# Attention mixed with a Mish network: the shifted copies of VectorE's exponential batches made in part by GpSimd, 1024 or 512 columns at a time

## The chip, the core and the metric

The kernel runs on one core of a Trainium2 chip. The metric is the device time of one execution, in microseconds, and lower is better. A run gives one such time; a kernel's figure is the median of its runs. Besides, one execution was taken by the hardware profiler; its page and its trace are what the numbers below come from. TensorE is called PE there (PEld is its weight load), VectorE DVE, ScalarE ACT, GpSimd POOL, and SP is the engine whose queue issues most DMAs.

## The reference

```python
def _A_ref(x, wqkv, wo):                       # x: 1 x 2048 x 640, 32 heads of 20
    qkv = (x @ wqkv).reshape(B, S, 3, H, Dh).transpose(2, 0, 3, 1, 4)
    scores = jnp.einsum("bhqd,bhkd->bhqk", q, k) * Dh ** -0.5
    p = softmax(scores)
    o = jnp.einsum("bhqk,bhkd->bhqd", p, v)
    return o.transpose(0, 2, 1, 3).reshape(B, S, D) @ wo
def _B_ref(x, w1, b1, w2):                     # w1: 640 x 1536
    h = x @ w1 + b1
    return (h * tanh(softplus(h))) @ w2
g = sigmoid((x * gate_w).sum(-1, keepdims=True))
out = g * _A_ref(...) + (1 - g) * _B_ref(...)  # both on the same x, bfloat16
```

The large part is the exponential of 32 x 2048 x 2048 scores.

## The kernel before

**Units and slots.** Scores are computed transposed, 128 keys by 512 queries of one head at a time; such a tile is a unit. A group is four heads (rows 0, 32, 64, 96 of the PE array) and one block of 512 queries. Three units make a slot, and there are 683 slots. For each slot PE writes three banks of PSUM (line 1324); two sets of three banks take turns, so the scores of slot s+2 can only be written when the exponentials of slot s have been read. ScalarE then makes the exponentials of a slot in one instruction (line 1345) into the ring ETS, and PE multiplies them with the values V, four heads at a time (line 1649), into one bank of sums per group.

**VectorE's units.** In some slots the third unit is not given to ScalarE. VectorE evicts it from PSUM instead (line 1391): it multiplies the score and adds a constant so that the result, stored as a 16-bit integer, is the bit pattern of an approximate exponential in f16. ScalarE's instruction of that slot then has 1024 columns in place of 1536. Four such units make a batch in a buffer of 2048 columns, called Y. To even out the error of the approximation, the batch is used three times: as it is (Y), with a constant subtracted from the integers (a copy in another buffer, U), and with a constant added (written over Y, called E; its values are multiplied by VW, a scaled copy of V made at line 1620). PE multiplies all three with V and adds them up. The two additions of a constant are the *shifts*. Before the change each shift is one VectorE instruction of 2048 columns (for batches of fewer units one of 1024 and/or one of 512), made by `shift` at line 1429. The buffers have the names of what else lies there: PADS, KT, QT, OTN, HB, REG, W2R.

**What else VectorE does.** It evicts projections, hidden units (line 1035) and outputs (line 1148) from PSUM, copies each group's sums to OUNG (line 1809), multiplies them by the broadcast reciprocals (line 1765) and computes Mish in eight steps on U (lines 1082 and 1085).

**GpSimd.** At the start it clears buffers. Later it makes the reciprocals of each group's sums, RR to the power of -1 (line 1831), which wait for a DMA that gathers the sums from OUNG; a DMA stores them in SUMS and four more spread them over BCT. In a few groups it also does the multiplication by the reciprocals.

**What sets the order.** All instructions come from one planner, written in Python, which runs when the kernel is built. It keeps a clock for each engine, adds instructions with an assumed cost each (the constants at the top of the file) and so fixes the order on every engine; nothing is decided on the chip. Dependences become semaphore waits, and each engine works through its queue in order. `choose(s)` decides whether slot s gives a unit to VectorE: it compares VectorE's planned backlog, and a correction from the table NUDGE for every eight slots, with limits (BEHIND, IDLE, and so on). `work` fills VectorE's planned gaps from lists of waiting jobs, `soon` among them, which holds the shifts; `settle` (line 493), called after each eviction, looks whether a job of `blend` (a Mish step) or `norm` (the multiplication by the reciprocals) can be given to GpSimd: only if it fits behind VectorE's last instruction of kind "L" (a shift, a Mish step or a multiplication, which work from SBUF to SBUF) and beside the evictions that follow in the plan. The job then waits for that last "L" instruction.

Of the kernel before, what the change touches and what calls it, by code (L numbers as in the profile page):

```python
# [11 lines left out]
I16 = mybir.dt.int16  # L12
# [27 lines left out]
OWE = -0.1  # L40
# [15 lines left out]
SPUN = 0.4  # L56
# [3 lines left out]
INVERT = 0.6  # L60
ASIDE = 1.3
ASIDE_1 = 1.2
APART = 0.1
AWAIT = 0.01
SHARE = 0.3
AWAIT_1 = 0
CALM_END = 60
# [3 lines left out]
LANES = 2  # L71
TAKEN = 3.6
LATE_OFF = 0.4
# [6 lines left out]
GIVE_BACK = 50  # L80
IDLE = 5
IDLE_2 = 6
# [3 lines left out]
NEAR = 0.2  # L86
STORED = 1.0
TALL = 0.1
BEYOND = 0.6
# [7 lines left out]
SPREAD = 1  # L97
# [3 lines left out]
BEHIND = 8  # L101
PATIENCE = 3
CATCH_UP = 10
BUSY = 0.9
CROWD = 1.05
MARGIN = 2.5
EAGER = 90
LOAD = 1.0
MISH = 4
GROUP = 2.5  # L110
LAST = 0
END = 55
SHIFT = 0.5
LAG = 40
SPARE = 3
WINDOW = 4.0
CALM = 1
# [10 lines left out]
OVER = 0.2  # L128
DIRECT = 3
FEW = 4  # L130
PART_DUE = 18
LAST_DUE = 13
# [21 lines left out]
NUDGE = [0.8, -4.2, -3.5, -3.7, 0.7, -0.7, -3.7, -1.5, -6, -1.5, -1.5, 2.3, 0.7, 0, -3.7, -1.5, 6, 0.0, 6, 0.7, -0.7, -5.9, 0.1, -0.7, 0, 3.7, -3, 1.5, 0.7, 0.7, 2.2, 6, 3.7, 1.5, 1, 2.2, 0.7, 2.1, 2.9, 2.3, 1.5, 6, 0.0, 2.9, 1.5, 0.7, -2.3, 1.5, 1.5, 1.5, 1.5, -2.3, 1.5, 0, 1.5, 0.8, 5, 0.0, 0.7, 2.9, 0.7, 1.5, 0, 4.5, 6, 0.7, -1.4, 1.6, 3, 0.8, 2.4, -0.8, 3.8, 0.0, 2.2, 5.7, 0.7, 5.2, 6, 0.7, 4.5, 0, 1.5, -0.7, -3, -1.5, -3]  # L154
# [116 lines left out]
def bass_gated_mix__softmax_full_mha__dense_activation_mish__prompt_kernel(  # L271
# [153 lines left out]
    def attention(pl, fast):  # L425
# [67 lines left out]
        def settle():  # L493

            while fast:
                for todo in (blend, norm):
                    job = todo[0][5] if todo and len(todo[0]) > 5 else None
                    ready = job and job[0]()
                    if not ready:
                        continue  # L500
                    line = pl.line
                    i = len(line)
                    while i and not line[i - 1][2]:
                        i -= 1
                    begin = max(ready.t1 + HOP, pl.now["pool"], line[i - 1][0])
                    while i < len(line) and line[i][0] <= begin:
                        i += 1
                    if begin + job[1] + APART <= pl.now["dve"]:
                        todo.popleft()
                        job[2](line[i - 1][1])  # L510
                        break
                else:
                    return
# [5 lines left out]
        def load(job):  # L519

            return job[0] * (SHARE if len(job) > 5 else 1)
# [5 lines left out]
        def work(until):  # L527
            while True:
                best = None
                lined = sorted([lane for lane in (*soon, blend) if lane], key=lambda lane: lane[0][3])  # L530
                for rank, todo in enumerate((norm, scaled, *lined, bg)):
                    for entry in todo if any(todo is lane for lane in soon) else islice(todo, 1):
                        cost, fn, dep = entry[:3]
# [874 lines left out]
        def close(batch):  # L1408
# [15 lines left out]
            where = spans(m)  # L1424
            each = QUAD * m / BATCH / len(where) + (0.0 if m == BATCH else 0.03)

            def shift(home, by, deps, after):
                for sp in where:
# [7 lines left out]
            def above():  # L1436
# [11 lines left out]
                def end(op):  # L1448
                    batch["parts"]["E"] = op
# [866 lines left out]
```

## Time and profile before

| what | value |
|---|---|
| median of 3 runs | 762.49 us (761.28 to 762.76) |
| the profiled execution's own time | 761.24 us |
| its span, first to last instruction | 759.4 us |
| instructions | 19104 |
| granted clock of TensorE | 0.999 |
| data read from and written to HBM | 35.57 MB, 7.51 MB (57 GB/s over the span) |

The span and the time of the same execution differ by 1.8 us. The page gives the busy time of each engine, groups of instructions by source line (busy time, mean duration of one, idle time of the engine ahead of them and what ended it), and the chain of waits that ended last. Other views of the same trace group by shape, cut the span into windows, or list instructions in order of time. An instruction's duration runs from its start to its end; on VectorE and ScalarE the next one can start before the last one has ended, so what one instruction takes from an engine that is never idle is the distance from its start to the next start.

### The profile page before, as it was taken

The numbers are of one execution on the slowest core, as the hardware profiler recorded it, in microseconds if no ns is written. First come the engines' busy times: TensorE is split into PE (matmuls) and PEld (weight loads), VectorE is DVE, ScalarE is ACT, GpSimd is POOL, SyncE is SP. The second block draws the span as 40 slices with busy tenths as digits, with TensorE's granted clock in tenths as the row PEclk, the third lists the DMA queues.
The fourth block names the chain that finished last, engine by engine and source line by source line (L and its number), as shares of the span: only waits on it lengthen the run. The fifth ranks groups of instructions, "written<-read, shape, count | busy, mean of one in ns | idle before, by whom it ended". The sixth has DMA issues, their size and how long they took to land.

```text
span 759.4 us, 19104 instructions
## 1 busy us (share of the span) xinstructions
PE 709.3 (93%) x7865; PEld 265.0 (35%) x7907; DVE 705.9 (93%) x1306; ACT 743.6 (98%) x714; POOL 123.2 (16%) x60
## 2 busy tenths in 40 slices
PE   8999999999999999999999899999998999999996
PEld 4433334333322333323333333333333333333332
DVE  4788899899899999998999999999999999999995
ACT  6999999999999999999999999999999999999996
POOL 8111101021110121202211202121022100111000
PEclk9999999999999999999999999999999999999999
DMA  8311311221133322241213222023122112010101
GB/s 182 109 56 48 103 52 34 66 65 59 49 94 98 104 57 81 57 133 37 64 44 111 74 67 58 29 68 86 48 68 69 55 41 71 21 33 14 31 7 39
DMA packets 80544, 49.03 MB, mean 65 GB/s; under 512 B 24602, under 2 KB 76690, under 8 KB 80450
## 3 DMA queue, kind: packets, MB, share of 16 engines
q1 hardware_dynamic: 80338, 47.71, 22.3%
q8 instruction: 65, 1.06, 0.6%
q14 instruction: 29, 0.24, 0.1%
q0 software_dynamic: 112, 0.01, 0.0%
HBM read 35.57 MB, written 7.51 MB: 57 GB/s over the span
## 4 chain that ended last, share of the span: by engine, by line
ACT 89%; PE 7%; DVE 2%; DMA 1%; issue 1%; SPq 0%; POOL 0%; POOLq 0%
ACT ETS L1345 86%; PE PS L1324 2%; ACT REG L1058 2%; PE PS L1649 2%; PE PS L562 2%; ACT W2R L1058 1%; PE PS L2043 1%; DMA WOQ<-in_A_wqkv_dram 1%; DMA REG<-in_B_w_dram 0%; DVE QT L1391 0%; PE PS L837 0%; DVE U L1082 0%; PE PS L901 0%; DVE HB L2168 0%; DVE OTN L1429 0%
## 5 line engine op out<-in xcount | busy, mean ns | idle before, releaser
L1345 ACT ACTIVATE ETS<-PS 128x1024 bf16<-128x1024 f32 (+1 forms) x683 | 722.6, 1270 | 4.0 <-PE PS L1324 3.2
L1324 PE MATMUL PS<-QT,KT 32*128 32x512 bf16 (+1 forms) x2112 | 268.8, 378 | 25.1 <-ACT ETS L1345 18.2
L1831 POOL TENSOR_TENSOR RR<-RR,NEG 128x16 f32<-128x16 f32 x29 | 91.4, 3151 | 499.4 <-DMA RR<-OUNG 492.5
L1649 PE MATMUL PS<-ETS,V_all 128*21 128x512 bf16 (+1 forms) x1624 | 167.0, 375 | 0.5 <-ACT ETS L1345 0.5
L1324 PEld LDWEIGHTS PS<-QT,KT 32*128 32x128 bf16 x2112 | 67.5, 91 | 234.1 <-ACT ETS L1345 182.1
L562 PE MATMUL PS<-XB,REG 128*128 128x256 bf16 (+3 forms) x703 | 78.5, 296 | 8.7 <-DVE HB L1035 2.6
L1391 DVE TENSOR_SCALAR QT<-PS 128x512 int16<-128x512 f32 x114 | 77.4, 688 | 2.7 <-PE PS L1324 1.8
L1391 DVE TENSOR_SCALAR OTN<-PS 128x512 int16<-128x512 f32 x112 | 76.0, 689 | 1.9 <-PE PS L1324 1.4
L562 PE MATMUL PS<-W2R,HB 128*32 128x320 bf16 (+1 forms) x666 | 73.8, 300 | 1.1 <-DVE OUTT L1148 0.5
L1391 DVE TENSOR_SCALAR PADS<-PS 128x512 int16<-128x512 f32 x90 | 61.2, 689 | 4.8 <-PE PS L1324 4.3
L562 PEld LDWEIGHTS PS<-XB,REG 128*128 128x128 bf16 (+1 forms) x719 | 38.3, 96 | 40.9 <-issue 28.0
L1649 PEld LDWEIGHTS PS<-ETS,V_all 128*21 128x21 bf16 x1624 | 40.2, 90 | 29.2 <-issue 25.0
L1085 DVE TENSOR_TENSOR U<-U 128x1024 f16<-128x1024 f16 x72 | 49.6, 689 | 0.2
L562 PEld LDWEIGHTS PS<-W2R,HB 128*32 128x32 bf16 (+1 forms) x666 | 33.5, 97 | 31.5 <-issue 14.9
L1391 DVE TENSOR_SCALAR KT<-PS 128x512 int16<-128x512 f32 x51 | 34.5, 687 | 4.5 <-PE PS L1324 4.1
L1391 DVE TENSOR_SCALAR REG<-PS 128x512 int16<-128x512 f32 x51 | 34.6, 688 | 1.6 <-PE PS L1324 1.5
L1035 DVE TENSOR_TENSOR HB<-PS,B1T 128x512 bf16<-128x512 f32 x48 | 33.1, 689 | 1.4 <-PE PS L562 1.3
L1082 DVE TENSOR_SCALAR U<-U 128x1024 f16<-128x1024 f16 x72 | 30.6, 425 | 0.5
L1429 DVE TENSOR_SCALAR QT<-QT 128x2048 int16<-128x2048 int16 (+2 forms) x52 | 27.7, 552 | 0.5 <-PE PS L1649 0.4
L1649 PE MATMUL PS<-QT,V_all 128*21 128x512 f16 x240 | 27.9, 384 | 0.0
L562 PE MATMUL PS<-XB,WOQ 128*32 128x512 bf16 (+1 forms) x136 | 25.1, 382 | 2.6 <-issue 1.6
L1429 DVE TENSOR_SCALAR OTN<-OTN 128x2048 int16<-128x2048 int16 (+2 forms) x42 | 25.8, 621 | 0.6 <-PE PS L1649 0.5
(174 smaller groups left out, 771.8 us busy)
## 6 DMA issues: line engine op xcount, KB each, us to landing
REG<-in_B_w_dram SPq DMA_DIRECT2D x36, 320.0 KB, 3.2
BCT<-SUMS SPq DMA_DIRECT2D x116, 64.0 KB, 2.0
W2R<-in_B_w_dram SPq DMA_DIRECT2D x12, 320.0 KB, 3.3
KT<-KS SPq DMA_DIRECT2D x28, 128.0 KB
QT<-QS SPq DMA_DIRECT2D x112, 20.0 KB
QS<-WOQ SPq DMA_DIRECT2D x16, 128.0 KB, 1.8
KS<-OTN SPq DMA_DIRECT2D x16, 128.0 KB, 1.8
W2R<-in_B_w_dram SPq DMA_DIRECT2D x1, 1920.0 KB, 8.4
```

What stands on the lines that cost most here:

```text
L562: op = e.matmul(PS[at, bank, cols], w[:, at], x, start=start, stop=stop, **({"tile_position": (0, i * rows)} if parts > 1 else {}))
L1035: ev = dve(lambda e: e.tensor_tensor(hb, PS[:, bank, :].rearrange("p (i t) -> p i t", i=2), bias, ALU.add), [last, b_load, *guarded, *b_re ...
L1058: ex = pl.add("act", lambda e: e.activation(U, h, AF.Tanh, scale=0.5, bias=-MISH_AT), [ev, u_free[0]], cost=0.95)
L1082: return lambda e: e.tensor_scalar(dst, src, *ops)
L1085: return lambda e: e.tensor_tensor(dst, one, two, ALU.mult)
L1324: op = pl.add("pe", lambda e, i=i, g=real(g), tile=tile, j=j, cols=cols, c=c, of_q=of_q: e.matmul(scores(s)[:, i, cols], KT[32 * j:32 * j ...
L1345: e_op[s] = pl.add("act", lambda e: e.activation(EXPS[:, at:at + n, :], scores(s)[:, 0:n, :], AF.Exp, scale=SCALE, bias=LIFT if fast else ...
L1391: ev = dve_by(lambda e: e.tensor_scalar(block(batch["y"], n, I16), scores(s)[:, 2, :], SCALE * ULPS, BIAS, ALU.mult, ALU.add), [s_op[s], * ...
L1429: op = pl.add("dve", lambda e, sp=sp: e.tensor_scalar(some_of(home, sp, I16), some_of(y, sp, I16), by, None, ALU.add), deps, cost=each, ki ...
L1649: lasts[n] = pl.add("pe", lambda e, v=v, j=j, src=src[:, cols], of_q=of_q, count=count: e.matmul(PS[32 * j:32 * j + EW, bank, of_q], v, sr ...
L1831: r = (pl.add("pool", lambda e: e.tensor_tensor(RR[:, :], RR[:, :], NEG[:, :].to_broadcast([P, 16]), ALU.pow), [got, m_neg], cost=INVERT) ...
L2043: pl.add("pe", lambda e: e.matmul(PS[:, bank, :], k[:, 0:P], k, start=True, stop=True), [free], cost=PASS, kind="S")
```

## The change

The shift of a batch is now a job (`queue_shift`) that can be done in pieces. Its buffer is cut into pieces of 1024 columns (512 for an odd unit). `run` is VectorE's turn: it does all the pieces that are left, as one instruction of 2048 columns if none has been taken. `aside` is GpSimd's turn: called from `settle`, it takes one piece off the end, if it fits beside VectorE's planned evictions at an assumed cost of BESIDE (1.05) or, for 512 columns, BESIDE / 2 + MOVED. What a batch's U, Y and E wait for is now a list of instructions, since pieces may come from two engines. `beside` is the test that `settle` had inside it before.

Most of the planner's constants and the table NUDGE have other values too: among them the assumed cost of GpSimd's reciprocals (INVERT 0.6 to 2.9) and of the DMA behind it (2.8 to 0.7), four lists of shifts for two (LANES), the limits of `choose` (BEHIND 8 to 8.5, IDLE_2 6 to 7), the times by which the last output parts are due (PART_DUE, LAST_DUE), and DIRECT: of the last groups, two and not three have their sums turned over by VectorE's transposes; the third one goes by GpSimd's reciprocals and the DMAs.

```diff
-INVERT = 0.6
+INVERT = 2.9
+BESIDE = 1.05
+MOVED = 0.1
+WITHIN = 0.1
-LANES = 2
+LANES = 4
-IDLE_2 = 6
+IDLE_2 = 7
-BEHIND = 8
+BEHIND = 8.5
-DIRECT = 3
+DIRECT = 2
...
-NUDGE = [0.8, -4.2, -3.5, -3.7, 0.7, ...
+NUDGE = [0.8, -4.2, -3.5, -1.5, 1.4, ...
...
 in settle():
                 else:
-                    return
+                    for lane in soon:
+                        moved = next((entry for entry in lane if entry[4](entry, lane)), None)
+                        if moved:
+                            break
+                    else:
+                        return
+
+        def beside(ready, cost):
+            line = pl.line
+            i = len(line)
+            while i and not line[i - 1][2]:
+                i -= 1
+            begin = max(ready.t1 + HOP, pl.now["pool"], line[i - 1][0])
+            while i < len(line) and line[i][0] <= begin:
+                i += 1
+            return line[i - 1][1] if begin + cost <= pl.now["dve"] else None
...
-            def shift(home, by, deps, after):
-                for sp in where:
-                    op = pl.add("dve", lambda e, sp=sp: e.tensor_scalar(
-                        some_of(home, sp, I16), some_of(y, sp, I16), by, None, ALU.add), deps, cost=each, kind="L")
-                after(op)
+            def queue_shift(first, home, by, deps, ready, after):
+                left = [sp for a, b, c, d in spans(m) for sp in ([(n, n + 1, c, d) for n in range(a, b)])]
...
+                def emit(eng, sp, cost, more=()):
+                    state["ops"].append(pl.add(eng, lambda e: e.tensor_scalar(
+                        some_of(state["home"], sp, I16), some_of(y, sp, I16), by(), None, ALU.add),
+                        [*state["deps"], *more], cost=cost, kind="L"))
+                def run():
+                    begin()
+                    some = [(0, 2, 0, 2)] if len(left) == 2 and left[1][3] == 2 else list(left)
+                    for sp in some:
+                        emit("dve", sp, each * (sp[1] - sp[0]) * (sp[3] - sp[2]) / m + 0.03 * (len(some) > 1))
+                    after(state["ops"])
+                def aside(entry, lane):
+                    op = ready()
+                    n = left[-1][3]
+                    if op is False or op is None or n < 2 and not MOVED:
+                        return False
+                    cost = BESIDE if n == 2 else BESIDE / 2 + MOVED
+                    dep = beside(op, cost + WITHIN)
+                    if dep is None:
+                        return False
+                    begin()
+                    sp = left.pop()
+                    emit("pool", sp, cost, [dep])
+                    if not left:
+                        lane.remove(entry)
+                        after(state["ops"])
+                    return True
...
-                    SUMS.ap().rearrange("j (r a) -> (j r) a", a=16), RR[:, :]), [r, *spread_last], "nr1", cost=0.4, tail=2.8)
+                    SUMS.ap().rearrange("j (r a) -> (j r) a", a=16), RR[:, :]), [r, *spread_last], "nr1", cost=0.4, tail=0.7)
```

In the changed file the lines have other numbers: 1361 is ScalarE's exponentials (1345 before), 1407 VectorE's evictions of its units (1391), 1456 the shifts (1429), 1881 the reciprocals (1831), 1699 the product with V (1649), 1340 the scores (1324).

**ScalarE, the first slots.** Rows with 1536 columns are slots that ScalarE has whole, those with 1024 columns slots that give a unit to VectorE. Seven rows of ScalarE's program, from the eighteenth exponential on, before:

```order
L1345 ACTIVATE ETS<-PS 128x1024 x3
L1345 ACTIVATE ETS<-PS 128x1536
L1345 ACTIVATE ETS<-PS 128x1024
L1345 ACTIVATE ETS<-PS 128x1536
L1345 ACTIVATE ETS<-PS 128x1024
L1345 ACTIVATE ETS<-PS 128x1536
L1345 ACTIVATE ETS<-PS 128x1024
```

and now, at the same place:

```order
L1361 ACTIVATE ETS<-PS 128x1024 x3
L1361 ACTIVATE ETS<-PS 128x1536
L1361 ACTIVATE ETS<-PS 128x1024
L1361 ACTIVATE ETS<-PS 128x1536
L1361 ACTIVATE ETS<-PS 128x1024 x3
L1361 ACTIVATE ETS<-PS 128x1536
L1361 ACTIVATE ETS<-PS 128x1024 x2
```

Slots that were whole have become slots with a unit for VectorE. Over the program there are 492 exponentials of 1024 columns and 191 of 1536 now, 475 and 208 before, and 491 evictions of VectorE's units for 474.

**VectorE and GpSimd, the second batch's U.** The batch was gathered in HB and its shifted copy U goes to KT. VectorE's rows around it before (the casts are projections):

```order
L1391 TENSOR_SCALAR KT<-PS 128x512
L755 CAST WOQ<-PS 128x512
L1391 TENSOR_SCALAR KT<-PS 128x512
L1429 TENSOR_SCALAR KT<-HB 128x2048
L755 CAST OTN<-PS 128x512
L1391 TENSOR_SCALAR KT<-PS 128x512 x2
```

and now:

```order
L1407 TENSOR_SCALAR KT<-PS 128x512
L771 CAST WOQ<-PS 128x512
L1456 TENSOR_SCALAR KT<-HB 128x1024
L1407 TENSOR_SCALAR KT<-PS 128x512
L771 CAST OTN<-PS 128x512
L1407 TENSOR_SCALAR KT<-PS 128x512 x2
```

The other 1024 columns are GpSimd's. Its rows behind the start-up work, where before there stood five reciprocals in a row and nothing between them:

```order
L1456 TENSOR_SCALAR KT<-HB 128x1024
L1456 TENSOR_SCALAR PADS<-KT 128x1024
L1881 TENSOR_TENSOR RR<-RR,NEG 128x16
L1456 TENSOR_SCALAR KT<-KT 128x1024 x2
L1456 TENSOR_SCALAR PADS<-PADS 128x1024
L1881 TENSOR_TENSOR RR<-RR,NEG 128x16
L1456 TENSOR_SCALAR HB<-HB 128x1024
```

Over the program GpSimd has 96 shifts of 1024 columns, 23 of 512, 9 Mish steps of 1024 columns, 30 reciprocals (29 before) and 7 multiplications by reciprocals (10 before). VectorE has 107 shifts of 2048 columns, 156 of 1024 and 27 of 512; before it had 190, 66 and 56.

**PE, the reader of that copy.** HB is Y of the same batch; the waits name the engine by its semaphore (f_dve, f_pool, f_act). Before:

```order
L1649 MATMUL PS<-HB,V_all 21x512 [waits f_dve]
L1649 MATMUL PS<-HB,V_all 21x512 x3
L1649 MATMUL PS<-ETS,V_all 21x512 x4
L1649 MATMUL PS<-KT,V_all 21x512 x4
L1324 MATMUL PS<-QT,KT 128x512 [waits f_dve,f_act]
```

and now:

```order
L1699 MATMUL PS<-HB,V_all 21x512 x4
L1699 MATMUL PS<-ETS,V_all 21x512 x4
L1699 MATMUL PS<-KT,V_all 21x512 [waits f_pool]
L1699 MATMUL PS<-KT,V_all 21x512 x3
L1699 MATMUL PS<-ETS,V_all 21x512 x4
L1340 MATMUL PS<-QT,KT 128x512 [waits f_dve,f_act]
```

PE now waits for GpSimd in front of the copy's four products, and the next scores stand behind them. Over the program 111 of PE's rows and 49 of VectorE's name GpSimd's semaphore; before it was 3 and 10.

111 lines of the change are left out of this document (55 added, 56 removed).

## The prediction

> **What bounds the kernel now.** The first part of the page gives the busy shares, the fourth the chain of work that ended last.
>
> ```profile
> PE 709.3 (93%) x7865; PEld 265.0 (35%) x7907; DVE 705.9 (93%) x1306; ACT 743.6 (98%) x714; POOL 123.2 (16%) x60
> ```
>
> The first row alone is not enough, since three engines are above 90%. The chain decides:
>
> ```profile
> ACT 89%; PE 7%; DVE 2%; DMA 1%; issue 1%; SPq 0%; POOL 0%; POOLq 0%
> ACT ETS L1345 86%; PE PS L1324 2%; ACT REG L1058 2%; PE PS L1649 2%; PE PS L562 2%; ACT W2R L1058 1%; PE PS L2043 1%; DMA WOQ<-in_A_wqkv_dram 1%; DMA REG<-in_B_w_dram 0%; DVE QT L1391 0%; PE PS L837 0%; DVE U L1082 0%; PE PS L901 0%; DVE HB L2168 0%; DVE OTN L1429 0%
> ```
>
> 86% of the span is ScalarE's exponentials, one behind the other. ScalarE is idle for 759.4 - 743.6 = 15.8 us in all. The view by windows of 20 us shows where; its columns are PE, PEld, DVE, ACT, POOL, each with its count of instructions, then clock and DMA.
>
> ```profile
> 0.00:20.00 20.00, 16.46 (x166) 8.76 (x171) 9.88 (x22) 13.15 (x15) 16.82 (x18) 1.00 0.88 193
> 140.00:160.00 20.00, 17.49 (x165) 6.08 (x168) 18.80 (x33) 19.97 (x20) 2.90 (x1) 1.00 0.21 60
> 540.00:560.00 20.00, 19.10 (x225) 7.00 (x226) 20.00 (x39) 20.00 (x20) 3.01 (x1) 1.00 0.15 44
> 740.00:759.00 19.00, 12.75 (x214) 6.02 (x204) 11.69 (x24) 12.76 (x11) 0.00 (x0) 0.95 0.12 38
> ```
>
> 6.85 us of the 15.8 are in the first window and 6.24 in the last, before the first scores and behind the last exponential; under 3 us are left for the 720 us between. So a shorter kernel needs less work on ScalarE. The work can go to VectorE, but VectorE has no room either: in the window at 540 it is busy for all 20 us. That is why GpSimd, at 3 us of 20, matters.
>
> **What one unit is worth to ScalarE.** The groups of line 1345 by shape (count, busy time, mean of one in ns):
>
> ```profile
> L1345 ACT ACTIVATE ETS<-PS 128x1024 bf16<-128x1024 f32 x475 | 483.5, 1140 | 2.0 <-PE PS L1324 1.5
> L1345 ACT ACTIVATE ETS<-PS 128x1536 bf16<-128x1536 f32 x208 | 323.1, 1568 | 2.0 <-PE PS L1324 1.7
> ```
>
> A unit that leaves ScalarE shortens one instruction from 1568 to 1140 ns, by 0.428 us. Both shapes overlap the next instruction in the same way, so the difference of the means is what the engine gains. The changed program has 492 exponentials of 1024 columns for 475: 17 units more, **17 x 0.428 = 7.3 us less on ScalarE**. The 24 Mish instructions of ScalarE are as before.
>
> **What VectorE pays and saves.** Here starts are needed, not durations. Instructions in order of time, VectorE's first, then GpSimd's one in that stretch, then a second stretch of VectorE:
>
> ```profile
> 164.38 0.68 DVE L1391 TENSOR_SCALAR W2R<-PS 128x512 int16<-128x512 f32 x1
> 164.98 0.42 DVE L1429 TENSOR_SCALAR QT<-HB 128x1024 int16<-128x1024 int16 x1
> 165.31 0.69 DVE L1391 TENSOR_SCALAR W2R<-PS 128x512 int16<-128x512 f32 x1
> 165.91 0.68 DVE L755 CAST WOQ<-PS 128x512 bf16<-128x512 f32 x1
> 166.51 0.68 DVE L1391 TENSOR_SCALAR W2R<-PS 128x512 int16<-128x512 f32 x1
> 167.11 0.42 DVE L1429 TENSOR_SCALAR HB<-HB 128x1024 int16<-128x1024 int16 x1
> ...
> 165.54 1.27 POOL L1765 TENSOR_TENSOR OTN<-OUNG,BCT 128x512 bf16<-128x512 f32 x1 [7.62 <-issue]
> ...
> 531.19 0.69 DVE L1429 TENSOR_SCALAR OTN<-OTN 128x2048 int16<-128x2048 int16 x1
> 531.79 0.29 DVE L1429 TENSOR_SCALAR REG<-QT 128x512 int16<-128x512 int16 x1
> 531.99 0.69 DVE L1035 TENSOR_TENSOR HB<-PS,B1T 128x512 bf16<-128x512 f32 x1
> ```
>
> From start to start an eviction takes 0.60, a shift of 2048 columns 0.60, of 1024 0.33, of 512 0.20. Shifts before: 190 x 0.60 + 66 x 0.33 + 56 x 0.20 = 147.0 us. Now: 107 x 0.60 + 156 x 0.33 + 27 x 0.20 = 121.1. That is 25.9 less, and not half, since a shift of 1024 costs more than half of one of 2048. Nine Mish steps that go to GpSimd save 9 x 0.33 = 3.0 (the same 1024 columns of 16 bits, priced as the shift). The 17 new evictions cost 17 x 0.60 = 10.2. The other moves on VectorE (three multiplications more, one pair of transposes less, one scaled copy of V in quarters) are a few instructions of such durations with both signs; I count them at nothing. **VectorE gets lighter by 25.9 + 3.0 - 10.2 = 18.7 us.** It isn't on the chain, so this is worth nothing by itself: it is the room in which the 17 units fit.
>
> **What GpSimd pays.** No row shows a shift on GpSimd. The nearest are its copies of 16-bit data, one input and one output (in the last place the mean in ns), a clear and the multiplication by the reciprocals:
>
> ```profile
> L669 POOL MEMSET QT<- 128x2048 bf16 x7 | 12.3, 1804 | 0.0
> L662 POOL COPY REG<-REG 128x400 bf16<-128x400 bf16 x1 | 0.5, 520 | 0.1
> L676 POOL COPY REG<-OUTT 128x5 bf16<-128x5 bf16 x1 | 0.2, 205 | 3.5 <-DMA OUTT<-in_gate_w_dram 3.5
> L1765 POOL TENSOR_TENSOR OTN<-OUNG,BCT 128x512 bf16<-128x512 f32 x10 | 12.7, 1268 | 78.1 <-issue 62.7 <-DMA BCT<-SUMS 15.4
> ```
>
> From 5 to 400 columns a copy grows by 315 ns, 0.80 ns a column, above 0.2 us: 1024 columns come to 1.0 us and 512 to 0.6. The clear, which only writes, gives 0.9 for 1024; the multiplication, with two inputs, 1.27 if an element read is what costs, 2.5 if a column is. I take 1.0, the copy being nearest, and keep 0.9 to 2.5. GpSimd then gets (96 + 9) x 1.0 + 23 x 0.6 = 119 us on top of 123, a third of the span.
>
> A piece is planned beside evictions. In the rows above GpSimd's instruction starts 0.23 us behind the start of the first eviction and covers three of them, and they keep their 0.60. At 1.0 us a piece ends 1.23 us behind that start, two evictions end at 1.20: it fits.
>
> The Trainium skill speaks against the change in GPSIMD Engine Reference, section 4.1 Engine selection: elementwise adds belong on VectorE, GpSimd being about half as fast with two inputs and roughly at line rate with one. The multiplication above, 1.27 us on GpSimd, agrees. By line rate at that page's 1.2 GHz a piece of 1024 columns would take an estimated 0.85 us, and the sum below would be the same.
>
> **PE and the DMAs.** 17 units more are used three times each in place of once: 34 products with V more, by fours. Nine idle-filling products are added (64 for 55). PE is idle for 50 us, so I cost them at nothing; without that cover they would be some 17 x 0.4 = 7 us at most, by the four products of 0.39 us in the view by time. One more group goes by GpSimd's reciprocals with six DMAs; nothing near the end waits for them that did not wait for VectorE's transposes. Start and end of the span keep their order, and their 13 us.
>
> ```profile
> 164.36 0.39 PE L1649 MATMUL PS<-ETS,V_all 128*21 128x512 bf16 x4
> 167.03 0.40 PE L1649 MATMUL PS<-ETS,V_all 128*21 128x512 bf16 x4
> ```
>
> **The sum.** 7.3 us off the chain, nothing late next: the profiled execution's 761.24 would be 753.9. That execution lies 1.25 under the median; from the median, 762.49 - 7.3 = **755.2 us**.
>
> **The waits that come in, and the rivals.** 111 of PE's rows name GpSimd's semaphore, 3 before, and 49 of VectorE's, 10 before. Behind a waiting product on PE stand the next scores, and ScalarE waits for those. How much PE can lose is in the view of waits (total us, times, longest): it reaches the scores early and waits for ScalarE.
>
> ```profile
> PEld PS L1324 <- ACT ETS L1345: 182.1, 464, 1.4
> ```
>
> That is 0.39 us each time. So a piece may be about 0.4 us late before ScalarE pays.
>
> *Rival 1, GpSimd late, slower.* GpSimd works in its order, and its reciprocals wait for a DMA. VectorE's copy of the sums and the reciprocals behind it, twice:
>
> ```profile
> 242.94 0.69 DVE L1809 COPY OUNG<-PS 128x512 f32<-128x512 f32 x1
> 250.20 2.90 POOL L1831 TENSOR_TENSOR RR<-RR,NEG 128x16 f32<-128x16 f32 x1 [25.23 <-DMA RR<-OUNG]
> ...
> 571.23 0.69 DVE L1809 COPY OUNG<-PS 128x512 f32<-128x512 f32 x1
> 573.90 4.86 POOL L1831 TENSOR_TENSOR RR<-RR,NEG 128x16 f32<-128x16 f32 x1 [11.16 <-DMA RR<-OUNG]
> 574.50 0.63 DVE L1429 TENSOR_SCALAR PADS<-QT 128x1024 int16<-128x1024 int16 x2
> ```
>
> 571.92 to 573.90 is the usual 2.0 us; the other took 6.6, so 4.6 late. Over the 29 pairs of such rows seven were clearly late, this one the most: 7 x 4.6 = 32 us is a bound, half of it a fair guess. Before, only BCT waited for them; now pieces stand behind. If 16 us of lateness reach PE in seven events, ScalarE loses 16 - 7 x 0.4 = 13 us, and the time is 755.2 + 13 = 768. The point of decision is 7.3 us lost. For it: the order of the queue, which nothing mends. Against it: the late ones lie in the first 360 us, with most of the DMAs, and a product stands behind other work. Chance 0.14.
>
> *Rival 2, GpSimd holds VectorE, no change.* At 1.27 us a piece runs 0.3 us past two evictions. If VectorE's next shift must wait for that, 105 x 0.3 = 31 us eat the 18.7 saved, VectorE is 13 us heavier, and where it is full (about half the windows) ScalarE loses 6.5: 755.2 + 6.5 = 761.7. At 2.5 us it would be far worse. The rows at 573.90 speak for a conflict: the reciprocals took 4.86 us, not 2.90, while VectorE worked from SBUF to SBUF; VectorE kept its pace there. Chance 0.09, most of it at 1.27.
>
> The Trainium skill, SBUF — State Buffer, section Who interferes with whom, says that a VectorE instruction in a two-port mode and a GpSimd instruction exclude each other for the whole of whichever began first, while one outside these modes with at most one input in SBUF doesn't contend. The row at 573.90 and the three undisturbed evictions agree. By that rule a piece of 1.0 us holds VectorE for 1.23 - 1.20 = 0.03 us, 3 us in all, and the sum stands.
>
> *Rival 3, waits also vanish.* Durations of exponentials show small stalls that idle time doesn't.
>
> ```profile
> L1345 ACT ACTIVATE ETS<-PS x683: 1005/1185/1763, 9.5 to 751.5; 128x1024 bf16<-128x1024 f32 x107, 128x1536 bf16<-128x1536 f32 x64
> ```
>
> One reaches 1763 ns, 0.2 above the mean of its shape. A VectorE with 18.7 us of room frees PSUM sooner; if that takes 4 us of such stalls, the time is 751. For it: VectorE full at 540. Against it: the idle time is put down to PE. Chance 0.10.
>
> **How the numbers follow.** Forecast 0.64 (752.5 to 758.5, some stalls gained or lost), rival 3 0.10, a gain half lost to waits (758.5 to 761) 0.03, rival 2 0.09, rival 1 0.14. Runs of this kernel tell 0.2%, 1.5 us, from no change. Faster: 0.64 + 0.10 + 0.03 = 0.77; the same: 0.09; slower: 0.14. The range is 750.5 to 763.5: it takes in rival 3 and rival 2 at 1.27 us and leaves out rival 1.
>
> **What would show it.** In the changed profile: the two groups of line 1361 with about 492 and 191 and the old means; ScalarE busy near 736; VectorE busy near 687; GpSimd's 1024 columns near 1.0 us and POOL near 240; idle time of ScalarE still near 16. Rival 1 would show as products with V, or shifts, that wait for POOL, and idle ScalarE behind them; rival 2 as shifts and Mish steps on VectorE with longer means. The forecast is wrong if idle time and stretched means of line 1361 take back more than 6 us.

## The result: 6.9% slower

| | before | changed |
|---|---|---|
| median | 762.62 us (761.28 to 763.50, 4 runs) | 815.12 us (813.37 to 816.99, 4 runs) |
| span of the profiled execution | 759.4 us | 812.0 us |
| granted clock of TensorE | 0.999 | 0.982 |
| shifts of 1024 and 512 columns on GpSimd | none | 96 and 23 |

The ratio is 1.069, 95% interval 1.0657 to 1.0724. The forecast was 755.2 us, and the range ended at 763.5.

From the first, fourth and fifth parts of the page of the changed kernel (busy time and share; the chain by engine; the exponentials with the idle time ahead of them):

```profile
PE 725.2 (89%) x7866; PEld 268.2 (33%) x7909; DVE 732.2 (90%) x1295; ACT 749.3 (92%) x714; POOL 453.5 (56%) x186
...
DVE 12%; PE 7%; POOL 4%; issue 1%; POOLq 0%
...
L1361 ACT ACTIVATE ETS<-PS 128x1024 bf16<-128x1024 f32 (+1 forms) x683 | 726.2, 1179 | 48.0 <-PE PS L1340 45.5
```

The chain could be followed back only over the last 24% of the span, from about 612 us on; in that part ScalarE isn't on it. GpSimd was to be busy for about 240 us and is for 453.5; VectorE was to come down to 687 and is at 732.2. Durations of exponentials overlap, so stalls are counted from start to start here and below: what one exponential or Mish step takes beyond 0.904 us (1024 columns), 1.330 (1536) or 0.947 (Mish). That sum was 14.0 us before and is 74.0 now. 60.0 more stalls, less the forecast 7.3, are 52.7; the span grew by 52.6. In this bookkeeping the 7.3 us came, and 60 went. The window that stood for a full VectorE before (PE, PEld, DVE, ACT, POOL, each with its count, then clock and DMA) now has both engines short of work:

```profile
540.00:560.00 20.00, 18.33 (x208) 7.03 (x205) 17.85 (x28) 19.27 (x20) 11.48 (x6) 1.00 0.25 72
```

The groups by shape, ScalarE's two and GpSimd's largest ones (busy us, mean ns of one):

```profile
L1361 ACT ACTIVATE ETS<-PS 128x1024 bf16<-128x1024 f32 x492 | 485.0, 1060 | 33.9 <-PE PS L1340 32.0
L1361 ACT ACTIVATE ETS<-PS 128x1536 bf16<-128x1536 f32 x191 | 282.3, 1487 | 14.1 <-PE PS L1340 13.5
...
L1456 POOL TENSOR_SCALAR OTN<-OTN 128x1024 int16<-128x1024 int16 x18 | 50.7, 2816 | 34.0 <-DVE REG L1456 10.1 <-DVE U L1101 6.3 <-PE PS L1699 4.9
L1098 POOL TENSOR_SCALAR U<-U 128x1024 f16<-128x1024 f16 x9 | 23.2, 2577 | 19.0 <-DVE U L1101 7.2 <-DVE QT L1456 6.4 <-DVE U L1098 4.3
```

The counts are the forecast ones, 492 and 191. A shift of 1024 columns takes GpSimd 2.78 us (median of 96, lowest 2.76), not 1.0; one of 512 takes 1.49, not 0.6.

What this does to the rest is seen in order of time, in one place. GpSimd's pieces, PE's products with V that use them, and ScalarE's exponentials:

```profile
288.98 2.82 POOL L1456 TENSOR_SCALAR PADS<-PADS 128x1024 int16<-128x1024 int16 x1
291.77 2.76 POOL L1456 TENSOR_SCALAR QT<-QT 128x1024 int16<-128x1024 int16 x1
...
291.86 0.40 PE L1699 MATMUL PS<-PADS,VW 128*21 128x512 f16 x4 [0.54 <-POOL PADS L1456]
294.59 0.40 PE L1699 MATMUL PS<-QT,VW 128*21 128x512 f16 x4 [2.12 <-POOL QT L1456]
...
295.49 1.02 ACT L1361 ACTIVATE ETS<-PS 128x1024 bf16<-128x1024 f32 x1 [2.79 <-PE PS L1340]
```

The pieces stand without a gap; each is later than the last. PE waits for the one (0.54 us) and then for the next (2.12), the scores behind that product come late, and ScalarE is idle for 2.79 us. Idle time is put down to PE, which itself waited for GpSimd. The view of waits (total us, times, longest) shows how often:

```profile
PEld PS L1340 <- ACT ETS L1361: 138.2, 338, 1.3
...
ACT ETS L1361 <- PE PS L1340: 45.5, 76, 2.8
...
PE PS L1699 <- POOL PADS L1456: 9.0, 8, 1.9
...
PE PS L1699 <- POOL QT L1456: 5.3, 7, 2.1
...
PE PS L1699 <- POOL OTN L1456: 4.4, 4, 2.3
```

With four more rows (2.3, 2.3, 1.2 and 0.4 us) products with V waited 24.9 us for pieces. PE's slack ahead of the scores, the first row, went from 182.1 to 138.2 us.

The second path goes by VectorE. Three of its instructions beside one piece of GpSimd:

```profile
109.56 2.77 POOL L1456 TENSOR_SCALAR KT<-KT 128x1024 int16<-128x1024 int16 x1 [1.55 <-DVE HB L1456]
...
110.60 0.41 DVE L1456 TENSOR_SCALAR KT<-KT 128x1024 int16<-128x1024 int16 x1
110.93 0.68 DVE L771 CAST OTN<-PS 128x512 bf16<-128x512 f32 x1
111.53 1.34 DVE L1456 TENSOR_SCALAR PADS<-KT 128x2048 int16<-128x2048 int16 x1
```

The eviction (L771) keeps its pace; the shift of 111.53 takes 1.34 us in place of 0.68 and ends 0.54 us behind the piece. Over the whole program VectorE's shifts of 1024 columns stand 0.463 us apart on the mean, 0.334 before, those of 2048 columns 0.692, 0.606 before, and evictions 0.603, as before. Summed over all instructions that follow each other directly, VectorE stands 44.5 us above the usual spacing of their shapes, the medians of before (before itself: 4.2). Below this is called **held time**.

A third thing comes with the stalls: the granted clock of TensorE, 0.982 on the mean in the table above. It is at one half in six stretches of 3.4 or 6.8 us, from 254.1, 295.0, 308.7, 431.6, 629.5 and 735.4 us on, 27.3 us in all; in the kernel before it falls only behind the last exponential. One of the stretches lies in this window, for which the view gives a clock of 0.83 (the last three numbers are clock, DMA share and GB/s):

```profile
300.00:320.00 20.00, 17.07 (x153) 5.92 (x146) 16.55 (x32) 14.79 (x15) 16.78 (x8) 0.83 0.26 73
```

In the 3.4 us ahead of each, PE had been busy for only 31 to 60%. Inside them a product of scores took 0.60 us by the median, elsewhere 0.38, and 19.9 of the 74.0 us of stalls touch them. PE's matmuls are busy for 725.2 us, against 711.0 for the same program in the first experiment below: some 14 us of PE's time, of which it isn't known how much reached ScalarE.

### The profile page after: what moved, and what is told of

It is laid out like the page before. It is cut to its first block, busy times and chain, and to the rows that moved or that the text cites. A ratio compares the mean times of both kernels' runs of the same rounds, so it can differ in the third digit from the quotient of the medians.

```text
span 812.0 us, 19348 instructions
## 1 busy us (share of the span) xinstructions
PE 725.2 (89%) x7866; PEld 268.2 (33%) x7909; DVE 732.2 (90%) x1295; ACT 749.3 (92%) x714; POOL 453.5 (56%) x186
## 5 line engine op out<-in xcount | busy, mean ns | idle before, releaser
L1340 PEld LDWEIGHTS PS<-QT,KT 32*128 32x128 bf16 x2112 | 69.0, 91 | 234.0 <-ACT ETS L1361 138.2
L1407 DVE TENSOR_SCALAR QT<-PS 128x512 int16<-128x512 f32 x122 | 82.5, 681 | 6.2 <-PE PS L1340 5.7
L1407 DVE TENSOR_SCALAR OTN<-PS 128x512 int16<-128x512 f32 x121 | 81.7, 681 | 5.8 <-PE PS L1340 5.2
L1456 POOL TENSOR_SCALAR OTN<-OTN 128x1024 int16<-128x1024 int16 (+1 forms) x22 | 57.9, 2631 | 43.7 <-DVE REG L1456 10.1
L1407 DVE TENSOR_SCALAR PADS<-PS 128x512 int16<-128x512 f32 x100 | 68.0, 684 | 15.7 <-PE PS L1340 15.1
L578 PE MATMUL PS<-W2R,HB 128*128 128x320 bf16 (+1 forms) x633 | 72.6, 301 | 2.3 <-DVE XB L1123 0.9
L1456 POOL TENSOR_SCALAR PADS<-PADS 128x1024 int16<-128x1024 int16 (+1 forms) x15 | 40.5, 2699 | 45.7 <-PE PS L1699 21.3
L1456 POOL TENSOR_SCALAR QT<-QT 128x1024 int16<-128x1024 int16 (+1 forms) x18 | 48.6, 2700 | 26.5 <-DVE U L1098 11.3
L578 PEld LDWEIGHTS PS<-W2R,HB 128*128 128x128 bf16 (+1 forms) x633 | 33.2, 97 | 33.0 <-issue 15.6
L1098 POOL TENSOR_SCALAR U<-U 128x1024 f16<-128x1024 f16 x9 | 23.2, 2577 | 19.0 <-DVE U L1101 7.2
L1456 DVE TENSOR_SCALAR OTN<-OTN 128x1024 int16<-128x1024 int16 (+2 forms) x52 | 29.3, 569 | 4.6 <-POOL PADS L1456 2.1
```

What stands on the lines that cost most here:

```text
L578: op = e.matmul(PS[at, bank, cols], w[:, at], x, start=start, stop=stop, **({"tile_position": (0, i * rows)} if parts > 1 else {}))
L1098: return lambda e: e.tensor_scalar(dst, src, *ops)
L1340: op = pl.add("pe", lambda e, i=i, g=real(g), tile=tile, j=j, cols=cols, c=c, of_q=of_q: e.matmul(scores(s)[:, i, cols], KT[32 * j:32 * j ...
L1407: ev = dve_by(lambda e: e.tensor_scalar(block(batch["y"], n, I16), scores(s)[:, 2, :], SCALE * ULPS, BIAS, ALU.mult, ALU.add), [s_op[s], * ...
L1456: state["ops"].append(pl.add(eng, lambda e: e.tensor_scalar(some_of(state["home"], sp, I16), some_of(y, sp, I16), by(), None, ALU.add), [* ...
```

## The experiments

All ratios are to before on the same chip. The edits are shown shortened. The first four runs share a median of before of 761.56 us.

**The price alone.** The same plan, instruction for instruction, but GpSimd's pieces multiply by 1.0 and then add.

```diff
-    some_of(state["home"], sp, I16), some_of(y, sp, I16), by(), None, ALU.add)
+    ops = (1.0, by(), ALU.mult, ALU.add) if eng == "pool" else (by(), None, ALU.add)
+    some_of(state["home"], sp, I16), some_of(y, sp, I16), *ops)
```

What suggested it was one row of the changed kernel, in order of time: of the nine Mish steps that GpSimd makes, the only one that multiplies and adds took 1.04 us.

```profile
520.35 1.04 POOL L1098 TENSOR_SCALAR U<-U 128x1024 f16<-128x1024 f16 x1 [0.36 <-DVE REG L1456]
```

> The changed program, instruction by instruction, but GpSimd's 119 shifts multiply by 1 and then add (two operations in one instruction) where they only added. Reason: the one Mish step on GpSimd that multiplies and adds took 1.04 us, the eight that only add 2.77. Theory (the price of the add-only instruction is the whole loss): 1024 columns near 1.05 us, GpSimd busy near 250 us, ScalarE's stalls back from 74 to some 14 to 20 us, time 754 to 760. Rival A (waits for GpSimd lose the time at any price, pieces being stuck behind reciprocals): over 775. Rival B (two operations cost no less): 2.8 us again, 815.

Measured: 765.40 us, ratio 1.0057 (1.0036 to 1.0078). The first part of its page and, from the groups by shape, GpSimd's largest group of pieces:

```profile
PE 711.0 (93%) x7866; PEld 265.3 (35%) x7909; DVE 696.8 (91%) x1295; ACT 739.6 (97%) x714; POOL 259.3 (34%) x186
...
L1457 POOL TENSOR_SCALAR OTN<-OTN 128x1024 int16<-128x1024 int16 x18 | 18.8, 1044 | 51.4 <-DVE U L1101 9.5 <-DVE REG L1457 9.2 <-DVE PADS L1457 7.2
```

A piece takes 1.044 us, GpSimd is at 259 us where 240 were forecast and VectorE at 697 where 687 were; held time is 10.8 us, and PE waits for GpSimd for 0.7 us in all. The time is 3.8 us above before of its chip; the changed kernel was 52.5 us above. So the price of one instruction, with nothing else altered, is some 49 of the 52.5 us. The time is above the 754 to 760 of the theory and well below rival A's 775. Something of 3 to 4 us is left: the span is 762.5, stalls are 23.5 us, 9.5 more than before, which is more than the 7.3 gained.

**The change's numbers without its pieces.** GpSimd gets no piece; the planner plans anew with the changed constants.

```diff
 def aside(entry, lane):
+    return False
     op = ready()
```

> The changed program with every shift on VectorE: GpSimd is never offered a piece, all other constants stay, and the planner, run again, gives VectorE 468 units (491 with the pieces, 474 before). Theory: the constants do no harm, 6 units less than before are 6 x 0.43 = 2.6 us more on ScalarE: 762 to 768. Rival C (the other constants or the new order lose the time): over 780.

Measured: 785.01 us, ratio 1.030 (1.0278 to 1.0322). That is in rival C's range, but it isn't a clean test: 17.3 of its 33.6 us of stalls are one accident between 600 and 640 us. TensorE's granted clock is at one half there from 599.7 to 623.6 us and from 630.4 to 637.3. ScalarE had not stalled ahead of 599.7; PE had been busy for 60% of the 3.4 us before. The longest stall, 9.1 us of waiting for PE, ends at 633.4. A plan made anew for other rules brings accidents of its own; why the clock fell here stays open. It serves as the base of the next run.

**Holding alone.** The plan of vector_alone, with 257 additions of 300 columns on GpSimd that nothing reads, where pieces would have stood. They are work that before doesn't have, and nothing waits for them.

```diff
-    begin()
-    sp = left.pop()
-    emit("pool", sp, cost, [dep])
+    for _ in range(n + 1):
+        dummy[0] = pl.add("pool", lambda e: e.tensor_scalar(
+            SCR[:, :], SCR[:, :], 1, None, ALU.add), [dep, dummy[0]], cost=0)
```

> As vector_alone, with the same order on VectorE, ScalarE and PE, and 257 add-only instructions of 300 columns on GpSimd beside it, in groups of two or three at the places where pieces fit; nobody reads what they write. It shows what GpSimd's access to SBUF alone takes from VectorE, without a wait for a piece. If being held is most of the loss: VectorE's shifts and Mish steps stretched as in the changed kernel, 790 or more. If late pieces are most of it: under 775.

Measured: 808.38 us, ratio 1.061 (1.0578 to 1.0642), 23.4 us above vector_alone.

```profile
L1485 POOL TENSOR_SCALAR SCR<-SCR 128x300 int16<-128x300 int16 x257 | 281.2, 1094 | 208.8 <-DVE OTN L1459 38.7
```

PE doesn't wait for GpSimd here at all. Held time went from 6.3 to 28.6 us, stalls from 33.6 to 55.5. The accident of vector_alone stands in this run too, at 622 to 653 us, so it isn't the difference. One part is not holding: two Mish steps of GpSimd stand behind the additions and are late, and VectorE waits 4.5 us for them. So 22 us of held VectorE and two late steps brought 22 us of stalls: holding does most of that by itself.

**Lateness alone.** two_ops, with powers that nothing reads ahead of each piece, so that pieces are late at their fast price.

```diff
+    dummy[0] = pl.add("pool", lambda e: e.tensor_tensor(
+        SCR[:, 0:5 * n - 1], SCR[:, 0:5 * n - 1], NEG[:, :].to_broadcast([P, 5 * n - 1]), ALU.pow), [m_neg, dep, dummy[0]], cost=0)
     emit("pool", sp, cost, [dep])
```

> As two_ops, with a power of 9 numbers a partition (4 for a piece of 512 columns) on GpSimd ahead of each piece, so that each piece comes some 1.7 us later while little is read from SBUF. It shows lateness without most of the holding. If late pieces are most of the loss: 785 or more. If being held is most of it: under 775.

Measured: 834.29 us, ratio 1.095 (1.0917 to 1.0983). It missed its aim. PE waited 37.6 us for GpSimd, but held time came back too, 36.6 us: a late piece lies no longer beside evictions but beside shifts (37 of VectorE's shifts began inside one of the 96 larger pieces, 17 in two_ops). Lateness brings holding with it, and the two can't be parted this way.

**What two_ops still lacks: the Mish additions.** Eight of the nine Mish steps on GpSimd (the text on record counts all nine) were still additions alone; the nine had a mean of 2.62 us. Here they multiply by 1.0 as well; the plan stays. For this run and those with four forms, under before's numbers and at the true price, before had 762.30 us.

```diff
-    ops = (one, two, ALU.mult, ALU.add) if two is not None else (one, None, ALU.add)
+    ops = (one, two, ALU.mult, ALU.add) if two is not None else (1.0, one, ALU.mult, ALU.add)
```

> two_ops with GpSimd's nine Mish additions (U + constant, 1024 columns, 2617 ns each there) written as multiply by 1.0 and add as well; the plan stays the same, instruction for instruction. Theory 1 (what is left of two_ops's +3.9 us over before are these nine: each runs 1.4 us longer than the 1.2 planned, holds VectorE's next shift or multiplication and stands in the chain with about 8 us): the nine take 1.04 us each, ScalarE's stalls fall from 23.5 to about 14 us, VectorE's f16 multiplications go from 613 to 600 ns, time about 756 to 759 us, ratio to before 0.992 to 0.997. Theory 2 (what is left is a plan that waits for GpSimd where it stands behind its reciprocals and their DMAs): the nine take 1.04 us, and the time stays at 763 to 766 us.

Measured: 759.62 us, ratio 0.9979 (0.9959 to 0.9998). The nine steps take 1.047 us, held time falls to 7.6 us. It is just past the upper end of what the first theory gave (756 to 759); stalls are 19.6 us and not 14, so it was not the whole rest.

**Which operations are slow.** The changed kernel with four forms in turn.

```diff
+    if eng == "pool":
+        ops = ((by(), None, ALU.add), (1.0, by(), ALU.mult, ALU.add), (by(), 1.0, ALU.add, ALU.mult),
+               (by(), 0.0, ALU.add, ALU.add))[turns[0] % 4]
+        turns[0] += 1
```

> The changed kernel with its 119 pieces on GpSimd in four forms by turns: add alone; multiply by 1.0, then add; add, then multiply by 1.0; add, then add 0.0. The plan stays the same. Theory 1 (an instruction with one operation is what is slow on GpSimd): 1024 columns take 2.78 us in the first form and 1.04 us in the other three. Theory 2 (only multiply-then-add is fast): the first, third and fourth take 2.7 us or more. Either way the time lies between two_ops (765) and the changed kernel (815): about 778 us by theory 1, about 800 by theory 2. VectorE's shifts that begin in the first third of a 2.78-us piece come out near 1.0 us, those that begin in its last third last until its end, and none is held beside the 1.04-us pieces that lie beside evictions.

Measured: 803.95 us in one run. Four pieces in a row of GpSimd's program (a third form, a fourth, a first, a second):

```profile
290.00 1.05 POOL L1462 TENSOR_SCALAR QT<-QT 128x1024 int16<-128x1024 int16 x1 [1.08 <-DVE W2R L1462]
292.24 3.80 POOL L1462 TENSOR_SCALAR PADS<-PADS 128x1024 int16<-128x1024 int16 x1 [1.19 <-DVE QT L1462]
296.01 2.77 POOL L1462 TENSOR_SCALAR QT<-QT 128x1024 int16<-128x1024 int16 x1
298.86 1.05 POOL L1462 TENSOR_SCALAR QT<-OTN 128x1024 int16<-128x1024 int16 x1
```

Medians over 22 to 26 pieces of 1024 columns: add alone 2.78 us, add and add 3.64, multiply and add 1.05, add and multiply 1.05. It is not the number of operations, and not the order. Neither theory had two additions at 3.64; their length may be what takes the time past the second theory's 800.

**Single operations.** The same, with four other forms. Two of them (multiply alone, maximum alone) leave the shift out of their pieces.

```diff
+        ops = ((1.0, None, ALU.mult), (-by(), None, ALU.subtract),
+               (by(), 1.0, ALU.add, ALU.mult), (0.0, None, ALU.max))[turns[0] % 4]
```

> The changed kernel with four other forms on GpSimd by turns: a multiplication by 1.0 alone and a maximum with 0 alone (both leave the shift out, so the pieces written by these two forms hold other numbers than they should), a subtraction alone, and add then multiply by 1.0. The plan stays. So far on 1024 columns: add alone 2.78 us, add and add 3.64, add and multiply 1.05 in either order. Theory 1 (an instruction that has a multiplication runs fast, any other slowly): multiplication alone 1.0 us, maximum and subtraction 2.8. Theory 2 (two different operations are what runs fast): all three single ones about 2.8 us. Theory 3 (only addition and subtraction are slow): maximum 1.0 us too.

Measured: 808.06 us in one run (before, here and in the last two experiments below: 761.63). Multiply alone 2.79 us, subtract 2.78, maximum 2.78, add and multiply 1.04 (medians of 22 to 26). Theory 2 holds: of the seven forms tried only those with two different operations, a multiplication and an addition, are fast.

**The pieces under before's numbers.** two_ops with all the numbers of the planner as before the change; 86 pieces come out.

```diff
-INVERT = 2.9
-LANES = 4
+INVERT = 0.6
+LANES = 2
...
-    [r, *spread_last], "nr1", cost=0.4, tail=0.7)
+    [r, *spread_last], "nr1", cost=0.4, tail=2.8)
```

> two_ops with every number of the planner as before the change (those that the diff alters, the list of nudges and the 2.8 us behind the reciprocals among them); the new rule that may place a shift on GpSimd stays, planned at 1.05 us, and 86 pieces come out of it. Theory 1 (the pieces at their planned price are worth what they save, and the changed numbers cost what two_ops is above before): about 755 to 760 us. Theory 2 (the pieces bring nothing on their own; a plan is only as good as its numbers were searched for, and any plan made anew lies some us above): 764 to 775 us.

Measured: 778.10 us, ratio 1.0208 (1.0193 to 1.0224). That is above the ranges of both theories. In this plan fast pieces bring nothing: it gives VectorE 469 units, fewer than the 474 of before, 12.0 us pass behind ScalarE's last exponential, 6.6 in before, and stalls are 26.0 us, spread over many places. That the changed numbers are needed is likely, not shown: it is one plan.

**The planner told the true price.** The changed kernel, additions alone, planned at 2.8 us; 22 pieces find a place.

```diff
-BESIDE = 1.05
+BESIDE = 2.8
```

> The changed kernel with GpSimd's pieces as they are (add alone, 2.78 us) but planned at 2.8 us in place of 1.05; 22 pieces of 119 then find a place beside evictions. Theory 1 (what made the changed kernel slow is the gap between the planned 1.05 us and the 2.78 us): few pieces, none late, VectorE's mean start spacing of 2048-column shifts back near 610 to 620 ns, time near that of the kernel without pieces (785) or below, 765 to 785 us. Theory 2 (GpSimd's instructions beside VectorE cost by themselves, planned or not): above 785, since 22 x 2.8 us more of GpSimd's time still collides with VectorE.

Measured: 786.80 us, ratio 1.033 (1.0313 to 1.0347). The time is 1.8 us above the first theory's range, where the second had put it, but the second theory's cause isn't there: VectorE's shifts of 2048 columns are back at 0.604 us, held time is 7.2 us, and PE waits 0.2 us for GpSimd. The 22 slow pieces, whose places were planned for their length, do little harm. Of its 35.4 us of stalls 14.6 are three long ones (4.7, 6.1 and 3.8 us); they are likely accidents of a new plan as in vector_alone, but their causes were not traced.

**The last wait that the change brought.** In mish_too the largest stalls of the middle stood at 118 us (2.4) and 123 (0.9); the second lies in a stretch at half clock, 120.4 to 123.8 us, behind the first. SyncE's queue there, in mish_too:

```profile
110.77 0.35 SPq L727 DMA_DIRECT2D KS<-OTN  x1
115.65 0.33 SPq L1885 DMA_DIRECT2D SUMS<-RR  x1
116.02 1.10 SPq L754 DMA_DIRECT2D KT<-KS  x2
```

The store of the reciprocals (SUMS from RR) waits until 115.65 for GpSimd, and a load of keys that needs nothing of them stands behind it. In this run the load goes first, there and in one other place; nothing else moves.

```diff
 def finish(self, new_sem):
+    for op in [op for op in self.ops if op.key == "nr1"]:
+        at = to = self.ops.index(op)
+        for n in range(at + 1, len(self.ops)):
+            other = self.ops[n]
+            if op in other.deps or other.eng == "sp" and other.key[:2] != "kr":
+                break
+            if other.eng == "sp":
+                to = n
+        self.ops.insert(to, self.ops.pop(at))
```

> mish_too, with SyncE's order changed in two places: where the DMA that stores GpSimd's reciprocals (SUMS from RR) stands directly ahead of a load of keys (KT from KS), the loads go first. Nothing else changes its place. Theory 1 (rival 1 of the prediction is at work here: the load of keys at 116.0 us waited for reciprocals that waited for their own DMA, and PE for that load): the 2.4 and 0.9 us by which ScalarE stalls at 118 and 123 us go, ScalarE's stalls in all fall from 19.6 to about 16 us, the time by 3 us to about 756.5, ratio to before about 0.993. Theory 2 (the load of keys is slow because of the other DMAs about it, not because of its place): stalls and time stay, 758 to 761.

Measured: 757.71 us, ratio 0.9948 (0.9933 to 0.9962): **0.5% under before**, with the interval clear of 1. SyncE's queue at the same place:

```profile
112.96 1.09 SPq L767 DMA_DIRECT2D KT<-KS  x2
115.65 0.32 SPq L1898 DMA_DIRECT2D SUMS<-RR  x1
```

The first part of its page:

```profile
PE 709.5 (94%) x7866; PEld 265.3 (35%) x7909; DVE 695.1 (92%) x1295; ACT 737.3 (98%) x714; POOL 246.3 (33%) x186
```

The keys are asked for 3.06 us earlier, both stalls and the stretch at half clock are gone, stalls in all are 16.6 us for 19.6, the span 755.1 for 757.8. The largest ones left stand at 250 and 251 us, 1.9 together, and have the other half of the same cause. From the chain of waits of keys_first (start, us, what):

```profile
243.96 4.67 DMA RR<-OUNG
248.63 0.07 issue
248.71 2.90 POOL RR L1895
251.60 0.08 issue
251.68 1.38 POOL W2R L1470
253.06 0.04 issue
253.10 0.40 PE PS L1713 x4
```

A DMA of 4.67 us makes the reciprocals late, and the piece behind them, and the product that needs it.

**Pieces ahead of the reciprocals.** As keys_first, but a piece that stands directly behind the reciprocals on GpSimd goes first, in some eleven places.

```diff
 def finish(self, new_sem):
+    for op in [op for op in self.ops if op.what == "invert"]:
+        at = self.ops.index(op)
+        sums = self.ops[at + 1]
+        for n in range(at + 2, len(self.ops)):
+            other = self.ops[n]
+            if op in other.deps or sums in other.deps:
+                break
+            if other.eng == "pool":
+                if other.what == "piece":
+                    self.ops[at:n + 1] = [*self.ops[at + 2:n + 1], op, sums]
+                break
```

> keys_first, with GpSimd's order changed as well: where a piece of a shift stands directly behind the reciprocals (about eleven places), the piece goes first, and the reciprocals and their store follow it. Theory 1 (pieces behind late reciprocals are late, like the one at 254.8 us, which PE waited 0.74 us for and which held a multiplication of VectorE for 0.8): the stalls of 1.2 us at 253 to 257 us go and some smaller ones, together 1 to 3 us; time 754 to 756. Theory 2 (the reciprocals are needed as soon as they can be had, or these pieces have no inputs earlier): what is won there is lost to later reciprocals, time as keys_first or up to 3 us above.

Measured: 763.14 us, ratio 1.0015 (1.0001 to 1.0028), 5.4 us above keys_first, more than either theory gave. The chain of waits shows the price:

```profile
251.16 3.08 POOL RR L1913
254.24 0.02 issue
254.26 3.16 DMA SUMS<-RR
257.44 0.32 SPq L1923
...
258.73 2.19 DMA BCT<-SUMS
260.92 0.02 issue
260.94 0.69 DVE OTN L1847
```

The reciprocals, put behind a piece that waited for its own inputs until 250.0, are late, and so are their two DMAs, the output that is scaled by them, and VectorE's order behind it: ScalarE stalls for 2.0 and 1.3 us at 260 and 263. The reciprocals are the more urgent of the two.

## Why the prediction was wrong

**The step that failed is what GpSimd pays.** The sum had (96 + 9) x 1.0 + 23 x 0.6 = 119 us. Measured in the changed kernel: 273.7 us for the 96, 35.8 for the 23, 23.2 for the nine Mish steps, 332.7 in all. The price was taken from copies, as the nearest row; a copy and an addition have the same shape but not the same speed there (the copy of 400 columns took 0.52 us, an addition of 300 columns in idle_adds 0.96 by the median). The other end, the multiplication's 2.5 us by columns, was nearer to 2.78, and it was named as far worse without being priced or given a place in the range. Both paths that were ranked as rivals opened at that price: VectorE held (rival 2), products waiting for late pieces (the chain of rival 1, without its DMA). How the 60 us of stalls part between the two, and what the halved clock adds, stays open, since late_pieces couldn't keep them apart; 40 us more held time, 24.9 us of waits and 14 us more of PE's time are the sizes seen, idle_adds shows that held time can turn almost fully into time, and late_pieces that lateness makes more of it.

The Trainium skill's sentence that one-input elementwise work runs on GpSimd at roughly line rate (GPSIMD Engine Reference, section 4.1 Engine selection), which the prediction let stand beside its 1.0, holds here for the multiply-and-add, 1.04 us, and not for an addition alone, 2.78. Its advice in the same place, to leave elementwise additions to VectorE, agrees with the changed kernel; keys_first, with its multiply-and-add on GpSimd 0.5% under before, goes the other way.

**ScalarE's gain was right.** 17 units at 0.428 us, 7.3: counts 492 and 191 as forecast, ScalarE busy 737.3 in keys_first (forecast: near 736). The stated check, that the means of line 1361 stay, was a poor one: they fell (1060 and 1487 ns) while the time rose, since exponentials that wait overlap less.

**VectorE's saving came in part, at the price of 1.0.** With pieces of 1.04 us it is busy for 694 to 697 us, where 687 were forecast; with 2.78 for 732. In keys_first 10.8 of the 18.7 us came: shifts are 23.4 us less (forecast 25.9), Mish steps 2.3 (3.0), evictions 12.0 more (10.2), and the multiplications and copies of V that the sum put at nothing cost 3.4 net of the transposes.

**Two evictions cover a piece: right at 1.04 us.** 1.04 + 0.23 is 1.27 and so 0.07 past 1.20, where 0.03 was said; in mish_too held time is 3.4 us above before.

**PE and the DMAs at nothing: nearly right.** PE is busy for 709.5 us in keys_first, before 709.3. But the store of the reciprocals in SyncE's queue cost some 3 us at one place (mish_too against keys_first); the sum had passed that queue over.

**Rival 1 exists, at less than half its price.** 13 us were worked out; the store ahead of the keys and the piece at 251 us come to about 3 and 2. With the right form of instruction and the keys first, the kernel comes to 757.7, 3.9 us under before of its chip: about half of the forecast 7.3. Its span is 4.3 us shorter than before's: 7.3 less 2.6 of stalls (16.6 for 14.0) and 0.4 at the ends.

## What to carry to other kernels

Before work moves to an engine, measure the very instruction there, operations included: with two operations in place of one, the same shift took 1.04 us and not 2.78, and that alone decided between 765 and 815 us. A plan that sets work beside other work is only as good as its durations: too long a piece is late itself, holds its neighbour, and makes the next one late. Where an unpriced instruction has bounds far apart, work out the time at both ends before the range is drawn.

## What the hardware showed that was not expected

GpSimd's instructions with an addition, a subtraction, a maximum or a multiplication alone took 2.78 us on 1024 columns of 16 bits, two additions 3.64, an addition with a multiplication 1.04; 512 columns 1.49, 1.93 and 0.62.

An addition of 2.77 us holds VectorE in two stretches only. VectorE's shifts of 1024 columns that began up to 0.7 us behind the addition's start ended some 1.3 us behind that start; ones that began between 1.0 and 1.7 us behind it were not held, and those from 1.5 us on lengthened the addition, which ended 0.89 us behind the end of the shift (the longest took 3.26 us); ones that began in its last 0.9 us were held to its end. The rows of 110.60 (not held) and 111.53 (held) above are of one addition. The Trainium skill says that the one that begins first has the shared ports for its whole instruction (SBUF — State Buffer, section Who interferes with whom). Pieces of 1.04 us kept to that: in late_pieces nearly all shifts that began in one ended 0.28 or 0.54 us behind it. The long additions did not; there the measurement decides.

The granted clock of TensorE went between full and one half, in steps of about 3.4 us, while PE still worked for more than half of the time: in vector_alone it fell at 599.7 us behind 3.4 us of which PE was busy for 60%. That share alone doesn't decide. In the changed kernel PE was busy for 52% of the 3.4 us ahead of 646.6 us, and the clock stayed full.
